# A transformer block scheduled by hand on one core: another order of the loads, another written order and slots, and window copies in two pieces

## The chip, the cores and the metric

One NeuronCore of a Trainium2 chip runs the whole program. The metric is device microseconds of one execution, the median of the runs. Profiles are of one execution each; a profiled execution has a span, from its first to its last instruction, and a time of its own, which is a little longer. PE is the matrix engine, ACT the scalar engine, DVE the vector engine, POOL the general-purpose engine, and SP the engine that here only issues DMA transfers.

## The reference

The block has two gated halves on 2048 tokens of 448 features. A condition vector `c` gives six modulation vectors. The first half is a layer norm, a modulation, and attention with 16 heads of 28 features over a window of 8 tokens at distance 2; the second is a layer norm, a modulation, another layer norm, and an MLP of width 1792.

```python
B, S, D, F, H, Dh, W, dil = 1, 2048, 448, 1792, 16, 28, 8, 2
mod = (silu(c) @ w_mod).reshape(1, 6, 1, -1)
sa, ca, ga, sb, cb, gb = (mod[:, i] for i in range(6))

h = layernorm(x) * (1 + ca) + sa
q, k, v = heads(h @ wqkv)
idx = pos[:, None] - arange(W) * dil            # earlier tokens only
logits = einsum('bhsd,bhswd->bhsw', q, k[idx]) * Dh ** -0.5
o = einsum('bhsw,bhswd->bhsd', softmax(masked(logits)), v[idx])
x = x + ga * (o @ wo)

h = layernorm(x) * (1 + cb) + sb
h = gelu(einsum(layernorm(h), w1) + b1)
x = x + gb * (einsum(h, w2) + b2)
```

## The kernel before

**Tiling.** The 2048 tokens stand as 8 tiles `p` of 128 rows, each row two neighbouring tokens, so that the distance of 2 becomes a distance of 1 within each of two halves `s`. The 448 features are four K tiles: three of 128 rows and a rest of 64, whose matmuls use half of the array's rows. Attention runs in 9 batches of 2·57 queries a half: logits are computed for blocks of 58 queries against 64 keys (`lt`, L733), exponentiated on ACT (L740), masked on DVE (L746), summed (`pd`, L755) and multiplied with v (`po`, L766); the denominators pass twice through ACT (L775, L777) and the scaled result is written by DVE (`qT`, L783) and projected with wo (L798). DVE adds it to x (L805).

**Stages.** Normalised tokens (`zy`, L471) get to feature-major form in two ways: by PE (`ptr`, L528) for the first units, by a DMA transpose otherwise; ACT or DVE then applies the modulation and writes `hT` (L497, L495). Q and K come from `hT`; the first unit's matmuls are at L563 and L541 with the 64-row rest at L547 and go through one PSUM tile `pq` for K and one for Q, each copied to `kT` and `qT` by a cast (L603). Later units produce token-major Q and K, copied to `zy` by ACT or DVE (L622, L623) and transposed by DMA (L625). V of a batch needs the windows of two blocks of 57 tokens, 64 tokens wide each, side by side: the first batch reads `hT` directly (L701), the others read a tile `hw` into which `windows` copies them (L684). Then come x1 = x + attention, two norms, a DMA transpose to `yT` (L829), the first MLP layer (L541 and L547 with `w_s`, `w_r`), gelu on ACT (L859), the second layer (L878), the last add on DVE (L884) and the store (L888). Batches 0–4 are followed by MLP tile 0, 5–6 by tile 1, 7–8 by tiles 2 and 3.

**What sets the order.** `Plan.add` records 703 numbered tasks. `Plan.emit` then issues them in the order of the table `ORDER`; a suffix puts a task on another engine (`:A` ACT, `:D` DVE, `:P` POOL) or takes its variant with the 64-row matmuls first (`:R`), and `k+f@m` issues `f` filler matmuls (`warm_w`, L379) ahead of task `k`. `SLOTS` gives each buffer its slot in its pool, PSUM among them. Each engine, and SP's queue of transfers, works in the order in which its tasks stand in `ORDER`. An argument `after` of `Plan.add` is a constraint on the order that a planner may choose; `emit` makes no instruction from it.

**Loads.** All loads but two tiny ones of `c` are issued by SP. `load` names each load's predecessor:

```python
queue.append(add("SP", 0.5, fn, reads=reads, writes=writes, bufs=bufs, fills=fills, after=queue[-1:], xfer=us,
                 name="load " + writes[0]))
```

The order of definition is x tile 0, `w_mod` for the attention's modulation (`wm_st`, 672 KB, and two rests `wm_r`), three K tiles of the QK weights (`wqk_st`, 225 KB each), x tile 1, two rests of the QK weights (`wqr_st`), x tiles 2–3, V weights, x tiles 4–7, the rest of `w_mod`, wo, and the MLP's. A QK weight is used after a "spread" has copied it into 32-column heads (`Wqk`, L436 on DVE, L438 on ACT, L439 on POOL; `Wqr`, L444 to L447).

Of the kernel before, what the change touches and what calls it, by code (L numbers as in the profile page):

```python
# [15 lines left out]
KT, KS = 4, 64  # L16
# [36 lines left out]
62 61 63+10@63 64 24 25 67 78 79 88:P 26 27 90:A 28 65 86 29 30 91 68+1@68 69 70 80 81 101+8@101 84 82 85:A 83 107  # L53
95+3@95 109 102 93:A 103 96 97 108 110 111 112 94:P 89:P 98 104 105:R 113 114 106 99 100 141 115:D 116 131 129 132 130
133 184 134 31 119:A 120:A 139 140 142 136 143 118:A 117:A 185 179 228:A 180 121 122:R 123 144 135 194 192 137 138 145
146 147 148 149:A 151:A 32 33 34 202 35 36 37 266 195 193 124 125:R 152 276 196 197 150 126 204 203 198 205 206 199
200:D 181 182 156 157 231 232 207 234 186 235 153:R 38 39 165 209 208 166 210 40 201 264 265 277 183 267 158 211 187
229+5@229 154:D 268 167 189 190 236 300 233 237 188 155 239 240 168 301:R 302 274 230:D 275 159 278 160 191 303 306 279
281 269 307 214 304 280 212 282 270 283 41 271 272:A 273 42 171 162:R 163 164 213 215 225 308 305 310 309 238 226 170
169 241 311 312 219:R 313 242 243 244 246 314 315 216 372:A 220 161 284:A 286:A 342 339 287:A 285:A 554:P 217 340 343  # L60
245 247 227 43 44 291:R 292 318 248 288 289 319 316 317 320 341 344 345 347 127 222 223 218 249 250 251 221 373:R 378
321 322 45 348 379 252 375 323 128 324 253 325 328 256 326 376 374 555 556 380 336:P 329 254 257 337:R 338 224 46 47
445:P 48 297 49 50 255 298 258 259 327 330 377 346 381 383 384 261 260 331 262:D 382 332 333 334:D 349 172 385 174 446:R
350 263 447 408 335 351 352 386 354 387 409 413 412 51 424:R 425 52 355 353 176 356 173 414 410 411 426 415 416 53 54
178 357 419:R 359 427 430 431 428 358 175 360 361 364 362 388 389 363 390 391 392 393 177 418 365 481 394 417 395 366
396 397 398 399 440 367 368 400 420 421 293 290 487 448 438 422 423 439 444 488 449 484 451 452 401 402 369 403 370:D
371 485 489 482:R 483 404 441 405 406:D 407 450 453 454 456 486 490 492 294:R 442 295 491 457 455 518:R 458 459 493 494
517 520 521 519 522 495 496 528 532 531 530 460 463 464 461 462 465 497 529 523:R 525 524 527 526 536 537 540 429 539
466 533 498 468 467 469 470 471 473 499 500 501 502 504 534 535 553 590 503 505 432 296 299 506 433 557 560 593 558 559
507 434 435 561 562 509 510 436 594 563 596 595 472 597 474 475 508 511 598 591:R 592 476 547 548 565 566 564 599 512  # L70
477 478 479:D 513 600 514 515 443 437 516 601 549 538 567 602 626 568 550 603 551 604 480 627 628 631 629 605 569 608
609 630 606 632:R 634 633 635 636 543 544 637 641 639 607 640 610 611 638 572 573 642:R 570 571 574 613 612 614 575 577
576 645 615 618 578 579 580 582 581 583 584 616 585 552 541 619 617 620 621 587 643 644 622 623 586 588:D 624 625 542
545 648 656 658 647 659 649 657 660 589 662 663 665 666 680 681 546 646 667:R 664 669 671 668 670 652 650 672 677:R 676
674 673 678 679 675 651 653 691 654 655 685 682 687 688 686 689 690 683 661 699 700 692 693 694 695 684 701 702 696 697
698
# [76 lines left out]
def kernel(  # L153
# [519 lines left out]
    def attention(i, tbl, prev_w1):  # L673
# [5 lines left out]
        if i not in DIRECT:  # L679
            hw = sb("hw", [128, KT, NS, 2, WK], BF16, "hw")  # L680

            def windows(copy):
                h = hT[:, :, kc:kc + WK]
                copy(out=hw.t[:].rearrange("p k s j c -> p (k s) j c"),  # L684
                     in_=bass.AP(h.tensor, h.offset, [h.ap[0], h.ap[1], [WQ, 2], [1, WK]]))
# [271 lines left out]
```

## Time and profile before

| what | value |
|---|---|
| runs | 171.32, 169.91, 171.61 us; median 171.32 |
| profiled execution | 169.7 us, its span 168.0 us |
| busy share of DVE, ACT, POOL | 68%, 63%, 27% |
| DMA | 18.26 MB, 33462 packets, 109 GB/s mean |
| granted TensorE clock, mean | 1.000 |
| gelu, L859, ACT | x56, 33.6 us |
| first MLP layer, L541 with `w_s`, PE | x168, 38.6 us |
| second MLP layer, L878, PE | x238, 44.4 us |
| Q and K, L541 with `wqk_st`, PE | x72, 15.3 us |

In the rows of the profile below, "a<-b" is output and input by the program's names, "128*128" the array's rows and columns in use, "xN" a count. A timeline row gives its start and its duration in us, the engine, the line and the operation; consecutive equal instructions are one row, and the brackets give the engine's idle time before and what ended it. The matmuls' durations overlap those of their neighbours, since they are pipelined, so that the pace of the matrix engine is read from one start to the next. SPq is SP's queue of transfers, where a row is the time of issuing.

### The profile page before, as it was taken

The page shows a single profiled execution, that of the slowest core. Times are in us where ns is not written, and L with a number is a line of the kernel's source. Part 1 is how long each engine was busy: PE and PEld are TensorE (multiplying, and loading weights), DVE is VectorE, ACT ScalarE, POOL GpSimd, SP SyncE. Part 2 cuts the span into 40 slices and gives each one's busy share as a digit, 9 for nine tenths or more (in the row PEclk, how much of TensorE's full clock was granted, in tenths as well). Part 3 has the DMA queues.
Part 4 walks back from the last instruction along what each step waited for, and adds up shares of the span by engine and source line. Part 5 has one row for each costly group of instructions (what it writes and reads, how often), then busy time and mean ns, then how long its engine had stood idle before and what let it go on. Part 6 is the DMA issues. An engine that isn't in the chain of part 4 may idle for free.

```text
span 168.0 us, 4975 instructions
## 1 busy us (share of the span) xinstructions
PE 162.4 (97%) x2116; PEld 84.7 (50%) x2116; DVE 114.4 (68%) x291; ACT 106.5 (63%) x146; POOL 45.7 (27%) x74
## 2 busy tenths in 40 slices
PE   7998999999999999999999999999999999999992
PEld 4785745565444643455544445464343554435571
DVE  7769999878999899997455979855998311002032
ACT  3369998899989835897992896880554404716000
POOL 7143320402616002931008210420123802900000
PEclk9999999999999999999999999999999999999999
DMA  5999949699997997008162000183000610000113
GB/s 159 342 286 385 238 97 155 169 116 149 297 220 181 177 279 124 4 0 96 37 116 68 0 4 4 55 91 92 4 0 0 118 62 0 4 0 0 55 64 102
DMA packets 33462, 18.26 MB, mean 109 GB/s; under 512 B 26395, under 2 KB 32480, under 8 KB 33440
## 3 DMA queue, kind: packets, MB, share of 16 engines
q1 hardware_dynamic: 33436, 17.95, 49.4%
q8 instruction: 16, 0.26, 0.6%
q14 instruction: 6, 0.05, 0.1%
q10 hardware_dynamic: 4, 0.00, 0.0%
HBM read 9.81 MB, written 1.84 MB: 69 GB/s over the span
## 4 chain that ended last, share of the span: by engine, by line
PE 91%; DMA 3%; DVE 2%; ACT 2%; issue 0%; DVEq 0%
PE p L878 26%; PE p L541 22%; PE pq L541 11%; PE pw L798 5%; PE pv L541 5%; PE p L547 4%; PE lt L733 4%; PE po L766 3%; PE pq L547 3%; DMA yT<-zy 3%; PE ps_c L379 2%; PE pd L755 1%; PE pv L547 1%; PE pv L701 1%; PE ptr L528 1%; PE pq L563 1%
## 5 line engine op out<-in xcount | busy, mean ns | idle before, releaser
L859 ACT ACTIVATE hm<-p,b_col 128x512 bf16<-128x512 f32 x56 | 33.6, 696 | 33.0 <-PE p L547 32.4
L878 PE MATMUL p<-w_s,hm 128*128 128x448 bf16 (+1 forms) x238 | 44.4, 342 | 0.0
L541 PE MATMUL p<-yT,w_s 128*128 128x512 bf16 x168 | 38.6, 379 | 0.3 <-DMA yT<-zy 0.3
L878 PEld LDWEIGHTS <-hm 128*128 128x128 bf16 x238 | 22.9, 98 | 19.2 <-issue 0.2
L467 POOL TENSOR_TENSOR rs_all<-tv_all,neg_half 128x2 f32<-128x2 f32 x22 | 17.0, 779 | 53.9 <-DVE tv_all L465 46.8
L884 DVE TENSOR_TENSOR x_all<-p,x1p 128x896 bf16<-128x896 f32 (+2 forms) x10 | 8.9, 901 | 30.6 <-PE p L878 30.6
L541 PEld LDWEIGHTS <-w_s 128*128 128x128 bf16 x168 | 15.7, 98 | 21.5 <-issue 4.1
L451 DVE BATCH_NORM_STATS2 stt<-x_all 128x6 f32<-128x448 bf16 x32 | 19.0, 614 | 0.7 <-DMA x_all<-in_A_x_dram 0.6
L740 ACT ACTIVATE et<-lt 128x928 bf16<-128x928 f32 x18 | 16.2, 947 | 3.1 <-PE lt L733 3.1
L836 POOL TENSOR_TENSOR x1p<-x_all,gbb_bc 128x448 f32<-128x448 bf16 x16 | 16.1, 1038 | 0.0
L541 PE MATMUL pq<-wqk_st,hT 128*128 128x448 bf16 x72 | 15.3, 353 | 0.0
L783 DVE TENSOR_TENSOR qT<-po,den 128x912 bf16<-128x912 f32 x9 | 9.9, 1106 | 6.8 <-ACT den L777 6.1
L798 PE MATMUL pw<-wo_s,qT 128*128 128x448 bf16 x64 | 12.9, 352 | 0.0
L746 DVE TENSOR_TENSOR et<-et,mask 128x928 bf16<-128x928 bf16 x18 | 11.3, 634 | 1.6 <-ACT et L740 1.6
L805 DVE TENSOR_TENSOR x_all<-pw,x_all 128x896 bf16<-128x896 f32 x8 | 8.5, 1084 | 4.2 <-PE pw L798 4.2
L622 ACT CAST zy<-pq 128x896 bf16<-128x896 f32 x11 | 10.0, 908 | 1.6 <-PE pq L547 1.4
L541 PE MATMUL pv<-Wv,hw 128*128 128x448 bf16 x48 | 10.5, 354 | 0.0
L814 DVE TENSOR_TENSOR h<-h,mod_bc 128x896 bf16<-128x896 bf16 x16 | 9.8, 622 | 0.3
L541 PEld LDWEIGHTS <-hT 128*128 128x128 bf16 x72 | 6.5, 98 | 6.4 <-issue 1.0
L777 ACT ACTIVATE den<-den,den_bias 128x928 f32<-128x928 f32 x9 | 9.5, 1068 | 0.2
L451 DVE BATCH_NORM_STATS2 stt<-h 128x6 f32<-128x448 bf16 x16 | 9.5, 618 | 0.2
L798 PEld LDWEIGHTS <-qT 128*128 128x128 bf16 x64 | 6.3, 98 | 5.9 <-DVE qT L783 0.3
(117 smaller groups left out, 190.1 us busy)
## 6 DMA issues: line engine op xcount, KB each, us to landing
w_s<-in_B_w_dram SPq DMA_DIRECT2D x7, 224.0 KB, 3.8
out_dram<-x_all SPq DMA_DIRECT2D x7, 224.0 KB
x_all<-in_A_x_dram SPq DMA_DIRECT2D x3, 448.0 KB, 6.0
wmod<-in_w_mod_dram SPq DMA_DIRECT2D x3, 448.0 KB, 9.7
w_s<-in_B_w_dram SPq DMA_DIRECT2D x3, 448.0 KB, 3.7
wqk_st<-in_A_wqkv_dram SPq DMA_DIRECT2D x3, 225.0 KB
wm_st<-in_w_mod_dram SPq DMA_DIRECT2D x1, 672.0 KB, 4.8
x_all<-in_A_x_dram SPq DMA_DIRECT2D x2, 224.0 KB
```

The source lines that it names most:

```text
L451: add("DVE", 0.53, lambda: nc.vector.bn_stats(out=stt[:, w, b, :], in_=src()), reads=reads, bufs=bufs, after=early if w == b == 0 else (), ...
L467: add("POOL", 0.55 + 0.17 * n, lambda: nc.gpsimd.tensor_tensor(out=r, in0=tv, in1=neg_half[:, 0:n], op=ALU.pow), reads=[f"tv{w}_{b0}", "ne ...
L541: nc.tensor.matmul(out(), lhsT=lhs(kt, slice(0, 128)), rhs=rhs(kt, slice(0, 128)), start=first and kt == 0, stop=not first and kt == KT - 2)
L547: nc.tensor.matmul(out(), lhsT=lhs(KT - 1, rows), rhs=rhs(KT - 1, rows), start=first, stop=not first, tile_position=(rows.start, 0))
L622: add("ACT", 0.80, lambda to=to, src=src: nc.scalar.copy(out=to(), in_=src()), bufs=[pq, st], reads=["zpad"], writes=[(st, 0)], name="evac ...
L740: exps.append(add("ACT", 0.83, lambda half=half, lt=lt: nc.scalar.activation(out=et.t[:, 2 * half:2 * half + 2].rearrange("p r m c -> p r ...
L746: nc.vector.tensor_tensor(out=ev, in0=ev, in1=mask[:], op=ALU.mult)
L783: nc.vector.tensor_tensor(out=qT[:, :, LEAD + q00:LEAD + q00 + 2 * WQ], in0=po.t[:, :, 0:NS * 4 * WQ].rearrange("p j (m c) -> p m j c", c=WQ),
L798: nc.tensor.matmul(pw.t[:, s, 0:D], lhsT=qT[:, KT * s + ft, LEAD + 128 * p:LEAD + 128 * p + 128], rhs=wo_s[:, ft, :], start=(ft == 0), sto ...
L836: add("POOL", 1.0, lambda n=n: nc.gpsimd.tensor_tensor(out=x1p.t[:, n, :], in0=xn(p, n), in1=gbb2_bc[:], op=ALU.add), reads=[f"x{p}", "gbb ...
L859: gelus.append(add("ACT", 0.585, lambda f=f, a=a, p1=p1s[g]: nc.scalar.activation(out=hm.t[:, f].rearrange("p n c -> p (n c)"), in_=p1.t[: ...
L878: nc.tensor.matmul(p2.t[:, n, 0:c1 - c0], lhsT=hm.t[:, f, n, q * 128:(q + 1) * 128], rhs=w2_s[:, f, c0:c1], start=(f == parts[0][0]), stop ...
```

## The change

Three things are changed: `load` lets every load from the fifth on depend only on the fourth; `windows` makes two copies of 128x512 in place of one of 128x1024; and the tables `ORDER` and `SLOTS` are others throughout, with the same 703 tasks.

```diff
     def load(fn, us, writes, bufs=(), reads=(), fills=()):
-        queue.append(add("SP", 0.5, fn, reads=reads, writes=writes, bufs=bufs, fills=fills, after=queue[-1:], xfer=us,
+        queue.append(add("SP", 0.5, fn, reads=reads, writes=writes, bufs=bufs, fills=fills, after=queue[-1:] if len(queue) < 4 else queue[3:4], xfer=us,
                          name="load " + writes[0]))
...
             def windows(copy):
-                h = hT[:, :, kc:kc + WK]
-                copy(out=hw.t[:].rearrange("p k s j c -> p (k s) j c"),
-                     in_=bass.AP(h.tensor, h.offset, [h.ap[0], h.ap[1], [WQ, 2], [1, WK]]))
-
-            add("DVE", 0.37, lambda: windows(nc.vector.tensor_copy), port=True, reads=["pads"] + [f"h{kt}_{p}" for kt in range(KT) for p in ps_],
+                for j in range(2):
+                    copy(out=hw.t[:].rearrange("p k s j c -> p (k s) j c")[:, :, j], in_=hT[:, :, kc + j * WQ:kc + j * WQ + WK])
+
+            add("DVE", 0.46, lambda: windows(nc.vector.tensor_copy), port=True, reads=["pads"] + [f"h{kt}_{p}" for kt in range(KT) for p in ps_],
                 bufs=[hw], fills=[hw], name="windows",
-                alt={"ACT": (0.93, lambda: windows(nc.scalar.copy)), "POOL": (1.1, lambda: windows(nc.gpsimd.tensor_copy))})
+                alt={"ACT": (1.12, lambda: windows(nc.scalar.copy)), "POOL": (1.18, lambda: windows(nc.gpsimd.tensor_copy))})
...
 ORDER = """
-3 0 1 2 11 12 4 9 5 17 14 18 15 55+14@55 19 20 21 10 7 8 13 6 71 22 23 92:P 87:P 73 74 16 56 57 58 72 75 59 60 76 77 66
+15 3 7 0 17 18 19 1 13 5 8 9 20 2 6 10 14 21 73 24 74 11 4 12 71 55+5@55 72 16 56 57 75 76 58 77 59 78 79 61 62 67 60
```

Lines of the changed kernel stand one or two numbers lower (the store is L886, the cast of Q and K L602).

**SP at the start of the program.** Before, the ten loads after x tile 0 follow their definition; `wqk_st` is a K tile of the QK weights, `wqr_st` their rest, `x_all` tokens, `Wv` the V weights:

```order
L336 DMA x_all_68<-in_A_x_dram 128x896
L343 DMA wm_st_135<-in_w_mod_dram 128x3x896
L346 DMA wm_r_157<-in_w_mod_dram 64x448 x2
L322 DMA wqk_st_160<-in_A_wqkv_dram 128x900 x3
L336 DMA x_all_68<-in_A_x_dram 128x896
L326 DMA wqr_st_237<-in_A_wqkv_dram 64x900 x2
L336 DMA x_all_68<-in_A_x_dram 128x2x896
L330 DMA Wv_74<-in_A_wqkv_dram 128x3x448
```

The changed kernel's queue at the same place:

```order
L335 DMA x_all_68<-in_A_x_dram 128x896
L342 DMA wm_st_127<-in_w_mod_dram 128x3x896
L345 DMA wm_r_129<-in_w_mod_dram 64x448 x2
L321 DMA wqk_st_154<-in_A_wqkv_dram 128x900
L335 DMA x_all_68<-in_A_x_dram 128x896
L321 DMA wqk_st_154<-in_A_wqkv_dram 128x900
L325 DMA wqr_st_225<-in_A_wqkv_dram 64x900
L321 DMA wqk_st_154<-in_A_wqkv_dram 128x900
L331 DMA Wv_74<-in_A_wqkv_dram 64x448
L325 DMA wqr_st_225<-in_A_wqkv_dram 64x900
L331 DMA Wv_74<-in_A_wqkv_dram 64x448
L335 DMA x_all_68<-in_A_x_dram 128x2x896
```

Token tile 1 moves ahead of two of the three QK weights, and one rest of these ahead of the last of them; the two small V rests move ahead of token tiles 2–3.

**ACT in the first QK units.** `kT` and `qT` are the casts of K and Q, `hT` the modulated tokens (the first three or four are of token tile 1), `et` the exponentials of batch 0, `vb0` its V. Before:

```order
L460 ACTIVATE tv_all_108<-mvs_107,eps_col_92 128x2
L462 ACTIVATE rs_all_109<-tv_all_108 128x2
L603 CAST kT_71<-pq_274 128x8x128
L603 CAST qT_70<-pq_290 128x8x128
L497 ACTIVATE hT_69<-ptr_338,mod_col_94 128x2x128
L497 ACTIVATE hT_69<-ptr_341,mod_col_94 128x2x128 x2
L497 ACTIVATE hT_69<-ptr_338,mod_col_94 128x2x128
L740 ACTIVATE et_397<-lt_353 128x928
L684 COPY hw_416<-hT_69 128x1024
```

In the changed kernel:

```order
L459 ACTIVATE tv_all_108<-mvs_107,eps_col_92 128x2
L445 COPY Wqr_73<-wqr_st_225 64x256
L461 ACTIVATE rs_all_109<-tv_all_108 128x2
L602 CAST kT_71<-pq_271 128x8x128
L496 ACTIVATE hT_69<-ptr_317,mod_col_94 128x2x128
L496 ACTIVATE hT_69<-ptr_314,mod_col_94 128x2x128
L496 ACTIVATE hT_69<-ptr_317,mod_col_94 128x2x128
L602 CAST qT_70<-pq_291 128x8x128
L714 CAST vb0_112<-pv_362 128x32x28
L738 ACTIVATE et_448<-lt_412 128x928
```

The cast of Q moves behind the modulation of token tile 1, and V's cast ahead of the first exponentials; the window copy leaves ACT at this place. On PE the K half of the first unit's products is now finished whole, then token tile 1 is transposed, then the Q half follows, then the first batch's V, then its logits; before, both halves were finished ahead of these transposes and the first half of the logits stood ahead of V. Fillers are 14, 10, 1, 8, 3 and 5 before and 5, 14, 13 and 5 now.

**SP at the end of the program.** Each row with `out_0_dram` is a store of finished rows; 128x896 is a whole tile of 224 KB, 128x224 a quarter of it. Before:

```order
L888 DMA out_0_dram<-x_all_68 128x896
L829 DMA_TRANSPOSE yT_2746<-zy0_97 128x8x128
L829 DMA_TRANSPOSE yT_2746<-zy4_101 128x8x128
L888 DMA out_0_dram<-x_all_68 128x896 x4
L888 DMA out_0_dram<-x_all_68 128x448
L888 DMA out_0_dram<-x_all_68 128x224 x2
```

In the changed kernel:

```order
L827 DMA_TRANSPOSE yT_2751<-zy3_100 128x8x128
L886 DMA out_0_dram<-x_all_68 128x896 x4
L886 DMA out_0_dram<-x_all_68 128x448
L886 DMA out_0_dram<-x_all_68 128x224
L886 DMA out_0_dram<-x_all_68 128x896
L886 DMA out_0_dram<-x_all_68 128x224
```

A store of a whole tile, that of tile 5 (task 661), now stands between the last two small ones. The window copies are on DVE three times, POOL three times and ACT twice before; now on DVE three times and on POOL five times, each as two instructions. Two more casts of token-major Q and K (L622 in the new numbering, L623 in the old) are on DVE and two fewer on ACT.

More of the change, by code (lines that the diff above doesn't have):

```diff
@@ L56 @@
[L56 to L60, printed above, removed]
@@ new lines @@
+157 154:D 231 232 233 234 235 264 207 165 41 166 236 209 201 187 188 208 210 158 189 190 159:R 160 300:P 237 239
+229+5@229 155 39 266 265 277 274 267 268 275 306 278 191 230 269 279 270 303 167 40 280 304 307 162:R 37 271 336 211 281
+272:D 215 214 127 212 213:A 240 282:D 238 168 38 273 128 308 305 50 283 301 302 216:R 241 309 161 163 311 445 310 170
+169 46 219:R 217:D 242 312 164 313 314 243 246 220 221 337 315 244 247 316 245 342 318 372:P 248 249 339 287:A 286:A
+284:A 285:A 288:R 317 319 320 321 338 291 343 218 45 344 340 289 375 251 250 378 341 323 252 376 379 322 225:R 44 253
@@ new lines @@
+453 406 442 489 454 482:R 486 456 457 590 294 490 483:D 371 492 295:D 407 493 517 491 455 458 518:R 521 522 520 494 495
+496 519 497 459 536 539 528 531 529 498 499 500 501 502 532 460 461 523:R 504 530 527 463 462 464 503 524 525 429 538
+505 506 533 534 465 507 591:R 592 537 508 509 510 466 468 526 511 467 469 540 535 512 428 470 473 471 472 296 514 434
+435 553 299 560 557 561 558 596 597 562 432 433 559 563 593 547 548 598 565 594 436 595 566 599 474 475 513 476 477 478
+515:A 601 564 600 602 626 567 603 549 550 551 604 605 608 609 479 568 606 607 610 569 437 516 480 570 627 629 630 628
@@ L77 @@
+572 632:R 631 633 634 541 542 637 635 636 642:R 543 571 573 574 575 576 577 578 641 639 643 579 582 580 581 638 611 613
+612 614 615 618 583 584 585 616 586 617 587 619 588:D 620 621 623 622 624:A 544 589 645 649 658 648 644 640 659 656 657
+443 660 545 625 662 663 666 667:R 665 664 671 668 669 670 652 653 672 676 674 673 680 677:R 647 678 679 646 684 682 681
+683 650 651 654 691 655 675 687 688 685 552 546 686 689 692 693 699 690 694 700 695 701 702 661 696 697 698
 """
```

28 lines of the change are left out of this document (9 added, 19 removed), and 12 rows, old and new, of the table SLOTS.

## The prediction

> **What bounds the kernel now.** I read the page's busy times and slices first, then every wait of PE that the view of waits lists.
>
> ```profile
> span 168.0 us, 4975 instructions
> PE 162.4 (97%) x2116; PEld 84.7 (50%) x2116; DVE 114.4 (68%) x291; ACT 106.5 (63%) x146; POOL 45.7 (27%) x74
> PE   7998999999999999999999999999999999999992
> ```
>
> ```profile
> PE ps_c L379 <- DVE warm_w L243: 1.3, 1, 1.3
> PE lt L733 <- ACT qT L603: 0.6, 1, 0.6
> PE ps_col L407 <- DVE wm_d L415: 0.3, 1, 0.3
> PE p L541 <- DMA yT<-zy: 0.3, 1, 0.3
> ```
>
> PE is busy 162.4 of 168.0 us. The 5.6 us left are the 1.3 us before its first instruction, three waits of 0.6 + 0.3 + 0.3 = 1.2 us, and about 3.2 us behind its last one. So the matrix engine bounds the kernel nearly throughout, and an order that keeps the same matmuls can win only from these 5.6 us, from fillers and from the cost of changing the shape of the array; it can lose anything. But busy PE time isn't all useful: some of the start is fillers, which PE does because nothing else is ready. The start, from the timeline of PE:
>
> ```profile
> 1.26 3.17 PE L379 MATMUL ps_c<-warm_w 128*128 128x256 bf16 x14 [1.26 <-DVE warm_w L243]
> 4.36 0.60 PE L386 MATMUL ps_c<-one,c_row 1*128 1x128 bf16 x4
> 4.90 1.62 PE L379 MATMUL ps_col<-warm_w 128*128 128x256 bf16 x10
> 7.95 0.61 PE L528 MATMUL ptr<-ident,zy 128*128 128x128 bf16 x8
> 8.40 1.04 PE L379 MATMUL pq<-warm_w 128*128 128x256 bf16 x8
> 9.27 0.38 PE L563 MATMUL pq<-hT,Wqk 128*128 128x256 bf16 x2
> ...
> 9.82 1.25 PE L563 MATMUL pq<-hT,Wqk 128*128 128x256 bf16 x10
> ...
> 13.07 0.62 PE L528 MATMUL ptr<-ident,zy 128*128 128x128 bf16 x8
> 14.28 0.44 PE L733 MATMUL lt<-qT,kT 28*64 28x58 bf16 x32 [0.59 <-ACT qT L603]
> 14.65 1.64 PE L701 MATMUL pv<-Wv,hT 128*64 128x448 bf16 x16
> 16.22 0.83 PE L541 MATMUL pq<-hT,Wqk 128*128 128x256 bf16 x6
> ```
>
> The third place to look at is the stage from 16 to 56 us, where the next engines are also nearly full (a window's row: stretch, its length, busy time of PE, PEld, DVE, ACT and POOL with counts, clock, DMA share, GB/s):
>
> ```profile
> 16.20:30.00 13.80, 13.80 (x280) 8.05 (x277) 13.64 (x38) 13.06 (x16) 3.42 (x7) 1.00 0.91 176
> 30.00:45.00 15.00, 15.00 (x332) 8.17 (x331) 12.55 (x26) 14.41 (x19) 4.13 (x6) 1.00 0.96 168
> 45.00:56.50 11.50, 11.50 (x260) 5.67 (x258) 11.29 (x32) 10.59 (x13) 4.56 (x5) 1.00 0.96 224
> ```
>
> There DVE is busy 13.64 + 12.55 + 11.29 = 37.5 of 40.3 us, 2.8 us short of full, and PE doesn't wait once.
>
> **The start.** Work to be done by the end of the first unit: the first half of QK unit 0, token tile 1's transposes, the second half, V, the logits. Before, the next QK unit begins at 16.22, with 0.44 us of batch 0's logits still to come behind it; after, these come ahead of it, so 16.66 is the comparable time. A walk through the new order, step by step: the modulation's matmuls wait for `silu_bc` and end about where they did, so the first transposes start at 8.05 (an estimate; 7.95 before) and take 0.45 (8.40 − 7.95). Then come 13 fillers at the pace of the row at 8.40, (9.27 − 8.40) / 8 = 0.109 us, to 9.9; before, two QK matmuls and all fillers are done at 9.82.
>
> ```profile
> 8.16 1.16 POOL L439 COPY Wqk<-wqk_st 128x512 bf16<-128x512 bf16 x2 [3.76 <-DMA wqk_st<-in_A_wqkv_dram]
> 12.30 1.01 ACT L603 CAST kT<-pq 128x1024 bf16<-128x1024 f32 x1 [1.13 <-PE pq L541]
> 13.21 1.02 ACT L603 CAST qT<-pq 128x1024 bf16<-128x1024 f32 x1
> 14.12 1.95 ACT L497 ACTIVATE hT<-ptr,mod_col 128x256 bf16<-128x256 bf16 x4
> ```
>
> POOL now makes three of these spreads instead of two, at 0.58 each, so the third ends near 8.16 + 3 × 0.58 = 9.9, in time for the second K tile. The stretch with the K half is 18 of the unit's 32 matmuls, 0.11 us each, and ends near 11.9. Tile 1's transposes (0.45) and the 14 others (1.5), with 0.2 for changes of shape, take PE to about 14.1, V (1.6 by its row) to 15.7. Meanwhile ACT casts K (1.0), modulates three quarters of tile 1 (0.49 each) and casts Q (1.0): 11.9 + 1.0 + 1.5 + 1.0 = 15.4, before V is done. The logits, 2 × 0.4 us, end at 16.5, and 16.66 is to be compared with it. The wait of 0.59 for the cast of Q goes, since V now covers it; what is late next are the fillers, which stand in the order whether or not data come sooner. Token tile 1 lands earlier, but DVE has it only behind the modulation columns and the casts behind PE's K half. I take 0. From the walk's roughest step, whether the third spread is in time, the bounds are ±0.6, the size of the wait that goes.
>
> **Shapes.** PE loses 0.10 us where a group ends with other rows in use: in the chain, six matmuls of the same size take 1.24 us ahead of a change and 1.14 without.
>
> ```profile
> 52.30 1.24 PE pv L541 x6
> 53.55 1.14 PE pq L541 x6
> ```
>
> Along the new order there are 88 such changes, before 90: −0.2.
>
> **The full stage.** DVE loses one cast of V (1.09) and two tail copies there later, and gets one more cast of token-major K (1.06), one more window copy, and a weight spread. Its own rows for the windows:
>
> ```profile
> L684 DVE COPY hw<-hT x3: 396/424/426, 26.6 to 100.0; 128x1024 bf16<-128x1024 bf16 x3
> L684 POOL COPY hw<-hT x3: 1037/1038/1042, 43.1 to 52.3; 128x1024 bf16<-128x1024 bf16 x3
> L684 ACT COPY hw<-hT x2: 1028/1055/1082, 16.8 to 38.4; 128x1024 bf16<-128x1024 bf16 x2
> L436 DVE COPY Wqk<-wqk_st 128x512 bf16<-128x512 bf16 x2 | 0.5, 286 | 0.0
> L719 DVE CAST vb<-pv 128x896 bf16<-128x896 f32 x1 | 1.1, 1092 | 0.0
> L623 DVE CAST zy<-pq 128x896 bf16<-128x896 f32 x1 | 1.1, 1059 | 0.0
> ```
>
> Two halves cost at least the 0.42 of the whole copy, and at most, by the row of another copy of 128x512, 2 × 0.286 = 0.57; I take 0.07 more than the whole, for halves that follow each other without a gap. The sum of DVE's tasks up to the last one that feeds the first MLP tile comes to +0.6 us, up to the batch's last scaling to +0.8. It fits into the 2.8 us that are idle, but the wait of 0.3 for `yT` shows that the chain of norms has no margin at its end. Nearest rows: −0.3 (that wait gone) to about +1.8 (below). I take 0, because in both orders the output projections of two tiles still stand on PE between the last scaling and the first MLP product. The first copies on POOL take 1.04 us each; PE needs them at V, more than a batch after, so they hide; without that cover each would cost up to its 1.04. On ACT two window copies (2.1 us) and two casts go: ACT isn't waited for in this stage, so no gain.
>
> **The end.**
>
> ```profile
> 163.00:165.00 2.00, 1.84 (x17) 1.40 (x15) 1.05 (x3) 0.00 (x0) 0.00 (x0) 1.00 0.62 229
> L888 SPq DMA_DIRECT2D out_dram<-x_all x10: 332/332/517, 87.6 to 165.3; - x10
> DMA to landing us min/median/max: 1.6/1.6/1.6
> 164.87 0.39 DVE L884 TENSOR_TENSOR x_all<-p,x1p 128x224 bf16<-128x224 f32 x1 [0.35 <-PE p L878]
> ```
>
> The last add ends at 165.26, and its store is issued at once, takes 0.33 to issue and lands 1.6 later. Now the 224 KB store of tile 5, issued before, stands between the last two small ones. Its rows have been ready for long, so it waits for the small store ahead of it, which comes from an add of 0.39 us that ends near 164.7; it then takes its 0.33 of SP's time until about 165.4, and the last store can only be issued from there: +0.1 to +0.33. If its bytes also go first through the 16 DMA engines, that is more: the DMA share of 0.62 in 2 us is 1.24 us for two whole tiles before, 0.62 each. So the ends are +0.25 (issue alone, with the queue's small steps) and +0.65; I take +0.45, halfway, since issue and bytes partly overlap. The Trainium skill's "DMA: Bandwidth & Descriptors", "Queues, rings and completion order", says that on each DMA engine the descriptors of one queue are taken in ring order; by it the sum would carry the upper end, 0.65. The profile has no case of a large store just ahead of the last one, so it can't say.
>
> **Sum**: 0 − 0.2 + 0 + 0.45 = +0.25 on the profiled execution's 169.7 us, so 169.95. The median of the runs, 171.32, is 1.6 above that execution, and I put the difference on the median: 171.57, rounded to 171.5.
>
> **Rivals.** A difference within 1%, 1.7 us, is about what a measurement of this kernel can't tell from no change.
>
> *Everything that waits goes (faster).* The waits of 0.6 + 0.3 + 0.3 go, four fillers fewer (41 to 37) are 0.44 at 0.109, the shapes 0.2, and the large store fits between two issues: −1.85, 169.5. For it: the wait list holds these waits and each has a changed step ahead of it. Against: fillers are cheap only if data are early, and each wait of the start ended at a step that has its own chain. 0.14.
>
> *Half pace at the start (slower).* PE's first 14 fillers took (4.36 − 1.26) / 14 = 0.221 us each, those at 8.40 0.109: the pace doubled in the second group, about 4.2 us after the first matmul. Only 5 fillers now stand ahead of `c`; they end at about 2.4, and PE is idle until `c` has landed. If the fast pace needs an unbroken run and counts again from a gap, the last gap being ahead of the transposes near 8.0, then it comes at 8.0 + 4.2 = 12.2: the 13 fillers cost 13 × 0.11 = 1.4 more, the K half 0.6 to 1.2 more, of which 0.5 lies in fillers that waited anyway: +1.8 net of the shapes, and +0.45 at the end, so 173.5. It decides if the half pace reaches past 9.5. Against it: the fillers of the row at 4.90 pass through a gap-free stretch, and 14 of the new ones fill the same. 0.13. The Trainium skill's "TensorE: Matmul & The Clock Gate", "Part 1: The HAM clock gate", has the clock go up after a busy window of about 3.4 us that runs freely; the rows' 4.2 us agree with it roughly, though the profile's mean granted clock is 1.000 with them in it. By it the 14 fillers would open the clock before 8.0, and this rival would not come about.
>
> *DVE's stage is late (slower).* The +0.8 on DVE lands in full on the wait for `yT`, and the two more window copies of POOL hold up short DVE rows:
>
> ```profile
> 43.14 1.04 POOL L684 COPY hw<-hT 128x1024 bf16<-128x1024 bf16 x1 [1.76 <-ACT hT L497]
> 43.88 0.32 DVE L465 TENSOR_SCALAR tv_all<-mvs 128x2 f32<-128x2 f32 x1
> L465 DVE TENSOR_SCALAR tv_all<-mvs x22: 158/169/714, 14.6 to 128.4; 128x2 f32<-128x2 f32 x22
> ```
>
> While POOL copied, that row took 0.32, not its usual 0.17, and the worst 0.71. Two copies at up to 0.54, less the part in DVE's idle time, are 0.5; the chain of scaling and `wo` meets the delay once more at batch 2, 0.5. Sum 0.8 + 0.5 + 0.5 − 0.2 + 0.45 = +2.0: 173.3. It decides when DVE's task sum grows by more than the idle time ahead of each consumer; speaking for it, DVE is at 13.64 of 13.80 in the first stretch, and against it, at 12.55 of 15.00 in the second. 0.22.
>
> *The loads come no earlier.* Tile 1's bytes share the DMA engines with the weights ahead of them, and if it lands no sooner the start is as before. That gives 0 there too, and it lies in the forecast.
>
> **The numbers.** Forecast, within 1%: 0.51, its own range 169.8 to 172.6 (start ±0.6, DVE −0.3 to the edge of 1%, end 0.25 to 0.65). Faster 0.14; slower 0.13 + 0.22 = 0.35. The range reaches down to the faster rival's 169.5 in part, 169.6, and up past both slower ones' 173.5 by a little, 173.8; what is left out is half of the faster case and the slower cases beyond their price.
>
> **What would show it.** Start: the second QK unit's first matmul at 16.66 ± 0.6, no wait for the cast of Q; half pace would show as fillers 0.22 apart behind 8.0. The full stage: the waits of PE keep at most 0.3 for `yT`; the third rival would show there as waits for `yT` or for scaled tokens of over 0.5. The end: from the last add's end to the end of the span, 168.0 − 165.26 = 2.7 before, 3.2 after. I am wrong if PE's busy time itself changes by more than 1 us, since the same matmuls at the same pace are assumed; or if a wait shows up in the MLP phases, where the order is also new and I have counted nothing.

## The result and the profile after

| | median, us | runs | lowest to highest |
|---|---|---|---|
| before | 170.82 | 20 | 169.76 to 173.82 |
| changed | 171.85 | 20 | 170.68 to 175.12 |

The ratio is 1.0061, 95% interval 1.0037 to 1.0085: 1.0 us slower (0.6 to 1.5), inside 1%. The highest times are those of a few slower executions, which the ratio leaves out. The profiled execution of the changed kernel took 171.82 us, its span 170.1. That of before, at 169.7, is faster than every one of its 20 other runs, while the changed kernel's is close to its median, so the spans (168.0 and 170.1) show about twice the difference of the medians. A second profile of the order before, in the experiment with split copies, has a span of 168.8.

The page of the changed kernel and all waits that the view of PE's waits lists:

```profile
span 170.1 us, 4976 instructions
PE 162.8 (96%) x2112; PEld 84.2 (50%) x2112; DVE 120.5 (71%) x295; ACT 103.9 (61%) x144; POOL 47.2 (28%) x80
PE 83%; DMA 6%; DVE 4%; SPq 2%; issue 1%; ACT 1%; POOL 1%; DVEq 0%
```

```profile
PE ps_c L378 <- DVE warm_w L242: 1.3, 1, 1.3
PE pq L546 <- DVE b_col L664: 1.1, 1, 1.1
PE pq L562 <- ACT hT L496: 0.8, 1, 0.8
PE ps_c L385 <- DMA c_row<-in_c_dram: 0.6, 1, 0.6
PE po L764 <- DVE qT L781: 0.2, 1, 0.2
```

PE is nearly as busy as before (162.8 against 162.4 us): the time went into waits, and of the chain (the third row of the page) 6% now runs through DMA and 2% through SP's queue, before 3% and none. The three old waits (the cast of Q, the modulation's weights, `yT`) are gone. New are a wait of 1.1 us in the full stage and one of 0.2 at `po` behind it, and at the start one of 0.8 and one of 0.6, in which PE waits for `c` behind the five fillers. The start, from PE's timeline:

```profile
1.26 1.25 PE L378 MATMUL ps_c<-warm_w 128*128 128x256 bf16 x5 [1.26 <-DVE warm_w L242]
3.09 0.60 PE L385 MATMUL ps_c<-one,c_row 1*128 1x128 bf16 x4 [0.58 <-DMA c_row<-in_c_dram]
3.62 3.17 PE L378 MATMUL ps_col<-warm_w 128*128 128x256 bf16 x14
7.77 0.61 PE L527 MATMUL ptr<-ident,zy 128*128 128x128 bf16 x8
8.21 1.58 PE L378 MATMUL pq<-warm_w 128*128 128x256 bf16 x13
10.55 1.32 PE L562 MATMUL pq<-hT,Wqk 128*128 128x256 bf16 x8 [0.75 <-ACT hT L496]
17.17 0.83 PE L540 MATMUL pq<-hT,Wqk 128*128 128x256 bf16 x6
```

The second QK unit begins at 17.17, 0.51 behind 16.66. The first MLP product begins at 63.24, before at 61.17, so that the stage between loses another 1.56; what follows it loses 0.03. The full stage, in the windows of before (the first one from its own second QK unit on):

```profile
17.17:30.00 12.83, 12.83 (x249) 7.76 (x242) 11.82 (x34) 11.21 (x15) 5.33 (x12) 1.00 0.70 142
30.00:45.00 15.00, 13.68 (x263) 6.82 (x261) 12.33 (x26) 12.51 (x16) 1.30 (x2) 1.00 1.02 190
45.00:56.50 11.50, 11.40 (x319) 5.90 (x319) 11.37 (x34) 10.43 (x13) 5.05 (x8) 1.00 1.11 261
```

PE loses 1.32 us between 30 and 45. DVE isn't fuller than before there (12.33 against 12.55), but the column of DMA is (it sums packet times that overlap, so that it can pass 1): 1.02 and 1.11, before 0.96 and 0.96, while the first stretch is emptier, 0.70 against 0.91. So transfers moved later. Which ones, SP's queue shows, with POOL's tail copy that completes token tile 5, and DVE's next work on it:

```profile
28.46 0.29 POOL L482 COPY zy<-zy 128x128 bf16<-128x128 bf16 x1 [4.37 <-DVE zy L470]
```

```profile
25.84 1.32 SPq L624 DMA_TRANSPOSE kT<-zy  x1
27.21 1.36 SPq L362 DMA_DIRECT2D wo_s<-in_A_wo_dram  x1
28.67 0.57 SPq L641 DMA_DIRECT2D mod_hbm<-mod_rows  x1
29.29 0.88 SPq L362 DMA_DIRECT2D wo_s<-in_A_wo_dram  x2
30.28 1.25 SPq L519 DMA_TRANSPOSE zT<-zy  x1
```

```profile
35.24 1.06 DVE L494 TENSOR_SCALAR hT<-zT,mod_col 128x512 bf16<-128x512 bf16 x3 [2.32 <-DMA zT<-zy]
36.31 0.17 DVE L664 CAST b_col<-pb 128x14 f32<-128x14 bf16 x1
```

Tile 5's tokens are ready at 28.75, and its transpose (`zT`, L519) is issued at 30.28: behind the store of the modulation rows and two loads of wo, a third of which SP had issued just ahead. DVE stands idle for 2.32 us until the transpose has landed, and PE's 1.1 us, put down to `b_col`, the last of the instructions that DVE does then, is the end of that. Before, the four loads of wo were issued together at a time when no transpose was due:

```profile
13.99 3.22 SPq L363 DMA_DIRECT2D wo_s<-in_A_wo_dram  x4
22.57 1.33 SPq L520 DMA_TRANSPOSE zT<-zy  x1
24.00 1.27 SPq L625 DMA_TRANSPOSE qT<-zy  x1
25.36 1.39 SPq L520 DMA_TRANSPOSE zT<-zy  x1
```

### The profile page after: what moved, and what is told of

Read it like the earlier page. It is cut to its first block, busy times and chain, and to the rows that moved or that the text cites. A ratio compares the mean times of both kernels' runs of the same rounds, so it can differ in the third digit from the quotient of the medians.

```text
span 170.1 us, 4976 instructions
## 1 busy us (share of the span) xinstructions
PE 162.8 (96%) x2112; PEld 84.2 (50%) x2112; DVE 120.5 (71%) x295; ACT 103.9 (61%) x144; POOL 47.2 (28%) x80
## 4 chain that ended last, share of the span: by engine, by line
PE 83%; DMA 6%; DVE 4%; SPq 2%; issue 1%; ACT 1%; POOL 1%; DVEq 0%
PE p L876 25%; PE p L540 22%; PE pq L540 9%; PE pw L796 7%; PE pv L540 4%; PE p L546 4%; DMA wqk_st<-in_A_wqkv_dram 3%; DMA zT<-zy 3%; PE lt L731 3%; PE po L764 2%; PE pq L546 2%; PE pd L753 1%; DVE et L744 1%; PE pv L546 1%; DVE stt L450 1%; PE pv L699 1%
## 5 line engine op out<-in xcount | busy, mean ns | idle before, releaser
L466 POOL TENSOR_TENSOR rs_all<-tv_all,neg_half 128x2 f32<-128x2 f32 x22 | 16.5, 757 | 45.7 <-DVE tv_all L464 36.8
L812 DVE TENSOR_TENSOR h<-h,mod_bc 128x896 bf16<-128x896 bf16 x16 | 11.3, 714 | 0.4
L683 POOL COPY hw<-hT 128x512 bf16<-128x512 bf16 x10 | 5.8, 613 | 18.9 <-PE pv L546 18.9
L773 ACT ACTIVATE den<-pd 128x928 f32<-128x928 f32 x9 | 8.5, 950 | 1.5 <-PE pd L753 1.4
```

Of the source, the lines that this page charges most:

```text
L466: add("POOL", 0.55 + 0.17 * n, lambda: nc.gpsimd.tensor_tensor(out=r, in0=tv, in1=neg_half[:, 0:n], op=ALU.pow), reads=[f"tv{w}_{b0}", "ne ...
L812: add("DVE", 0.55, lambda vec=vec, op=op: nc.vector.tensor_tensor(out=h2.t[:], in0=h2.t[:], in1=vec.unsqueeze(1).to_broadcast([128, NS, D] ...
```

## The experiments

Ratios are to the kernel before, timed on the same chip. "QK" is the start of the second QK unit, "MLP" that of the first MLP product, both from the profile of the run; orders that have half of the first batch's logits behind QK are to be read 0.44 later in the column QK (marked *).

| run | ratio, 95% interval | span, us | QK | MLP |
|---|---|---|---|---|
| before | | 168.0 | 16.22* | 61.17 |
| changed | 1.0061 (1.0037 to 1.0085) | 170.1 | 17.17 | 63.24 |
| a1_loads | 1.0108 (1.0070 to 1.0147) | 171.4 | 17.40 | 64.52 |
| a2_store | 1.0071 (1.0037 to 1.0105) | 170.1 | 16.40 | 63.24 |
| a3_zt5 | 1.0070 (1.0028 to 1.0112) | 169.9 | 16.36 | 63.02 |
| b1_split | 0.9976 (0.9956 to 0.9995) | 168.8 | 16.60* | 62.02 |
| c2_po3 | 1.0085 (1.0059 to 1.0111) | 170.0 | 16.79 | 63.14 |
| c3_both | 1.0054 (1.0024 to 1.0083) | 169.1 | 16.71 | 62.19 |
| g_122 | 1.0221 (1.0194 to 1.0249) | 172.7 | 17.89 | 65.89 |
| d1_fill | 1.0118 (1.0086 to 1.0151) | 170.2 | 17.65 | 63.36 |
| f1_wo | 0.9992 (0.9974 to 1.0010) | 168.4 | 17.08 | 61.53 |
| f2_all | 1.0010 (0.9990 to 1.0031) | 168.9 | 17.08 | 62.00 |
| f4_lt | 1.0008 (0.9989 to 1.0027) | 168.5 | 16.31* | 61.71 |
| m1_wo | 1.0127 (1.0103 to 1.0151) | 170.4 | 16.24* | 62.73 |

In these kernels a line of the code can stand one or two numbers off those above.

**a1_loads**: the first loads of the changed kernel in the order of before. Its tasks on SP, with tile 1's statistics and ACT's copy moved so that they don't block:

```diff
-wqk0, x1, wqk2, wr0, wqk1, wvr1, wr1, wvr0, x2
+wqk0, wqk1, wqk2, x1, wr0, wvr1, wr1, wvr0, x2
```

> The changed kernel with the first loads in the order of before (three QK weights, then token tile 1, then the QK rests), tile 1's statistics on DVE behind tile 0's modulation, and ACT's copy of the QK rest behind it too. Theory: tile 1's tokens and a QK rest ahead of the last QK weight are what delays the first QK products (0.75 us wait at 9.80, 0.11 at 11.15); the second QK unit then begins at 16.5 to 16.7 instead of 17.17 and the time falls by about 0.5 us, ratio to before near 1.003. Rival: tile 1's tokens come 1.5 us later and its transposes become what is waited for; the second unit stays at 17.2 or later, ratio 1.006 or more.

QK at 17.40, ratio 1.0108: no gain, so the theory fell. The rival's numbers came, but not its mechanism: PE didn't wait for tile 1, but 0.30 us for ACT's copy of the QK rest. Eight profiles share the changed kernel's order up to there (a2, a3, c2, c3, g, f1, f2 and its own); they have QK at 16.36 to 17.89, on average 16.94. Before, b1 and m1 share the other one, at 16.66 to 17.04 with the 0.44, on average 16.79. What the eight differ in is when the weights land: POOL began the first of its spreads at 10.21 in g, which has the latest QK, at 9.18 in the changed kernel's own profile, and at 8.46 to 8.77 in the four with the earliest (a2, a3, c2, c3).

**a2_store**: the end of the written order with the large store back in its place.

```diff
-693 699 690 694 700 695 701 702 661 696 697 698
+693 699 690 661 694 700 695 701 702 696 697 698
```

> The changed kernel with the large store of tile 5 moved back ahead of the last three small ones. Prediction's term: 0.45 us faster (0.25 to 0.65), and the span ends about 2.3 us behind the last add instead of 2.73. Rival, from the profile of the changed kernel, where the end behind the last add is as long as before: the large store is issued and gone before the last add ends, so nothing changes, 0 within 0.1 us in the profile.

The span is 170.1 again, and in the changed kernel the end behind the last add is what it was before:

```profile
166.99 0.39 DVE L882 TENSOR_TENSOR x_all<-p,x1p 128x224 bf16<-128x224 f32 x1 [0.95 <-PE p L876]
```

167.38 to 170.1 is 2.7, and 165.26 to 168.0 was 2.7. DVE now waits 0.95 between the last two adds, 0.35 before, and in that gap, at 166.45 to 166.87, the large store is issued. The rival held: 0.

The same profile shows something else. The first wait in the full stage is there (1.0 us), and a second, at `po`, put down to "issue", a name for waiting on nothing that the profile shows:

```profile
PE po L765 <- issue: 1.0, 1, 1.0
PE pq L547 <- DVE b_col L665: 1.0, 1, 1.0
```

```profile
53.36 0.39 PE L754 MATMUL pd<-et,ones_k 64*32 64x464 bf16 x8
53.57 1.09 PE L765 MATMUL po<-et,vb 64*32 64x57 bf16 x107
55.70 0.27 PE L765 MATMUL po<-et,vb 64*32 64x57 bf16 x21 [1.04 <-issue]
```

QK was 0.77 us earlier than in the changed kernel's own profile, and yet the first MLP product starts at 63.24 in both: the gain was swallowed at 55.70, where PE goes on in both.

**a3_zt5**: the transpose of tile 5 (task 211) ahead of wo's loads.

```diff
-229+5@229 155 39 266 265
+229+5@229 155 211 39 266 265
...
-167 40 280 304 307 162:R 37 271 336 211 281
+167 40 280 304 307 162:R 37 271 336 281
```

> The changed kernel with the DMA transpose of token tile 5 issued ahead of four other transfers of SP (two pieces of wo and the store of the modulation rows among them). Theory: it was queued behind them, issued 1.5 us after its tokens were ready; it is now issued near 28.8 instead of 30.28, lands by 33.7, and PE's wait of 1.13 us at 35.4 falls to 0.3 or less; about 1 us faster, ratio to before near 1.000. Rival: one DMA engine that is busy with a 16 KB instruction packet, or the full DMA engines, set the landing; the wait stays at 0.8 or more, or comes back within the next batch, and the time falls by 0.3 us at most.

The wait of 1.1 went, and the first output projection began at 38.26 instead of 39.75 in a2 at the same QK. The time didn't fall: transposes of Q and K of the next batches, which also stand behind these loads on SP, were late instead, and the stop at `po` was there.

```profile
PE po L765 <- issue: 0.9, 1, 0.9
PE ps_c L386 <- DMA c_row<-in_c_dram: 0.8, 1, 0.8
PE lt L732 <- DMA qT<-zy: 0.7, 1, 0.7
PE lt L732 <- DMA kT<-zy: 0.6, 1, 0.6
```

So the place of one transpose isn't the cause; the rival was right that the wait comes back.

**b1_split**: before, with the two copies of the changed `windows`, and nothing else.

> The kernel before with the window copies split in two and nothing else. Forecast: hidden, within 0.2 us of before; a pair on DVE takes 0.49, on POOL about 1.1 to 1.2, on ACT 1.2 to 1.3 us. Rival: the longer holds on DVE and POOL delay the chain of norms in the full stage, 0.3 to 0.8 us slower, seen as a longer wait for yT.

0.9976, no slower. The rows of the copies are 0.286 us each on DVE, 0.616 on POOL and 0.634 on ACT; the two of a pair overlap by up to 0.15, so that from the start of the first to the end of the second a pair takes 0.46 to 0.49, 1.17, and 1.12 to 1.17:

```profile
L684 DVE COPY hw<-hT x6: 261/286/293, 26.9 to 101.1; 128x512 bf16<-128x512 bf16 x6
L684 POOL COPY hw<-hT x6: 612/616/618, 43.9 to 53.9; 128x512 bf16<-128x512 bf16 x6
L684 ACT COPY hw<-hT x4: 602/634/663, 17.1 to 39.5; 128x512 bf16<-128x512 bf16 x4
```

A pair is a little longer than the one copy, by 0.07 us on DVE, 0.13 on POOL and 0.09 on ACT on average, and hidden. That it is a gain I don't claim: the interval ends just below 1, the span isn't shorter, and f4_lt, which has the split too, is at 1.0008.

**c2_po3**: in the changed order, `po` of batch 3 (task 346) behind one group of V matmuls; **c3_both**: that, tile 5's transpose as in a3_zt5, and one MLP load (46) behind the transposes of Q and K of batches 3 and 4.

```diff
-381 382 256 53 328 326 329 327 330 292 223 554:P 290 346 555:R 254 383
+381 382 256 53 328 326 329 327 330 292 223 554:P 290 555:R 346 254 383
```

> The changed kernel with the second of two batches' `po` products in a row moved behind one group of V matmuls. Theory: PE runs out of instructions there. In three of four profiles of this order it stops at the same instruction (the 108th of 128 `po` matmuls), 1.2 to 1.5 us after a 16 KB instruction packet has ended, whatever came before; the packet is fetched 256 PE instructions ahead, and pd, po, po are 272 short ones in a row. With 16 slow matmuls between, the stop of about 1.0 us goes and the time falls by 0.5 to 1.0 us, ratio to before 1.001 to 1.004. Rival: what the profile calls issue is a wait for data that comes when it comes; the stop only moves to V or to the output projection, ratio 1.006 to 1.007 as before.

> The changed kernel with token tile 5's transpose issued early, one MLP weight load moved behind the transposes of Q and K of batches 3 and 4, and the second `po` moved as in the kernel of this name. Theory that the two causes (SP's order ahead of the transposes, and the fetch) are separate and together make up the loss: both waits of about 1 us go, the waits for Q and K of 0.70 and 0.57 fall below 0.4 each; ratio to before 0.995 to 1.000. Rival: the stage is bound by the DMA transposes themselves, so PE waits for the next of them; ratio 1.002 to 1.006.

In c2 the stop is gone, as in every profile with that edit (c3, f2), and PE waits 0.3 us at V instead; two more changes of shape would cost 0.2 at the 0.10 of the prediction (an estimate). From QK to the first MLP product it takes 46.35, against 46.84 in a2: half a microsecond, of which the runs show nothing, since the ratio of 1.0085 isn't below the changed kernel's. The gain that was expected of it didn't come, though the stop went. c3 brings this to 45.48 and the span to 169.1, with waits of 0.08, 0.32 and 0.31 left. So the waits fell as its theory had it, but the ratio, 1.0054, is in the rival's range and isn't told apart from the changed kernel's.

**g_122**: the start of the changed order and its slots, up to the second QK unit, followed by the order of before, with split copies.

> The kernel before with the start of the changed one (its order up to the first half of the second QK unit, its first loads among it) and split window copies. Theory: the start is worth 0.3 to 0.6 us (second QK unit at 16.4 in two profiles of the changed order, against 16.66 to 17.04 for the same work before) and the loss comes later, from the order behind it; ratio to before 0.995 to 0.998, with the split copies' 0.998 in it. Rival: the gain at the start is lost to DVE and the transposes in the full stage, ratio 1.000 or more.

It fell, far: QK at 17.89, behind a wait of 1.4 us for the spread weights, 0.5 + 0.2 at the next transposes, 0.5 at a `po` (at 32.4) and 1.1 for `yT`. About 1 us of the loss is the late start, which the order itself doesn't explain, since seven others with it are earlier; the rest comes behind it, in the order of before. Why it waits there wasn't tried further; the start is at any rate not a part that brings a gain ahead of any order.

**d1_fill**: 14 and 10 fillers in place of 5 and 14.

```diff
-55+5@55 ... 63+14@63
+55+14@55 ... 63+10@63
```

> The changed kernel with 14 fillers ahead of the condition's matmuls and 10 ahead of the modulation's, as before, in place of 5 and 14. If the gap of 0.6 to 0.9 us behind 5 fillers delays the full pace (0.215 us from filler to filler until 6.4 us or later in the changed kernel, until about 5.5 before), the full pace comes by 5.7 again; the modulation's matmuls then start at 6.4 instead of 6.7 to 6.9, and the second QK unit 0 to 0.3 us earlier. Rival: the pace doesn't decide there, since the matmuls wait for the condition and for the spread weights; second QK unit at 16.4 or later, time unchanged within 0.2 us.

The pace does depend on them:

```profile
1.26 3.17 PE L379 MATMUL ps_c<-warm_w 128*128 128x256 bf16 x14 [1.26 <-DVE warm_w L243]
4.36 0.54 PE L386 MATMUL ps_c<-one,c_row 1*128 1x128 bf16 x4
4.83 1.26 PE L379 MATMUL ps_col<-warm_w 128*128 128x256 bf16 x10
7.28 0.61 PE L407 MATMUL ps_col<-silu_bc,wm_st 128*128 128x32 bf16 x18 [1.19 <-DMA wm_st<-in_w_mod_dram]
```

The second group runs at 1.26 / 10 = 0.13 us or less from its first filler on, where in the changed kernel all 14 fillers at 3.62 are (6.65 − 3.62) / 14 = 0.22 apart. But the modulation's matmuls waited 1.19 us for their weights here, the first QK products 0.8 for the spread weights, and QK came at 17.65, as the rival had it. The time wasn't lower (1.0118), so the pace doesn't decide; why this one is slower than the changed kernel the runs don't settle.

**f1_wo**: the changed kernel with only the four loads of wo back behind the modulation weights and the load of b1. SP's queue:

```diff
 load wmod2 (four pieces), load b1
+load wo 0, 1, 2, 3
 transposes zT4, tq2, tk2
-load wo 2
 store of the modulation rows
-load wo 3, load wo 0
 transpose zT5, broadcast of the modulation rows
-load wo 1
 transpose zT6
```

> The changed kernel with the four loads of wo issued behind the modulation weights, near 14 us, as before, in place of 27 to 32 us between the DMA transposes. Theory: these loads are what token tile 5's transpose queues behind on SP; its issue falls from 30.28 to near 29, the wait of 0.95 to 1.13 us at 35 us falls to 0.3 or less, the first output projection starts at 38.3 to 39 instead of 39.75 to 40.7; the stop in the `po` products stays (about 1 us, or more, since PE comes there earlier), so the time gains 0 to 0.4 us. Rival: the transposes set their own time on the DMA engines; the wait stays at 0.8 or more.

0.9992: the whole loss is gone, where 0 to 0.4 us of it had been expected. SP's queue, DVE's work on tile 5 and the complete list of PE's waits:

```profile
13.26 4.97 SPq L363 DMA_DIRECT2D wo_s<-in_A_wo_dram  x4
...
27.25 0.56 SPq L642 DMA_DIRECT2D mod_hbm<-mod_rows  x1
28.68 1.24 SPq L520 DMA_TRANSPOSE zT<-zy  x1
```

```profile
32.75 1.05 DVE L495 TENSOR_SCALAR hT<-zT,mod_col 128x512 bf16<-128x512 bf16 x3
```

```profile
PE ps_c L379 <- DVE warm_w L243: 1.3, 1, 1.3
PE ps_c L386 <- DMA c_row<-in_c_dram: 0.9, 1, 0.9
PE pq L563 <- POOL Wqk L439: 0.3, 1, 0.3
```

Behind the start no wait is listed at all. The transpose is issued 1.6 us earlier, and DVE has tile 5 2.5 us earlier and without an idle moment ahead of it; the 0.9 beyond the issue mean that it also landed sooner behind it. From QK to the MLP it takes 44.45, before 44.51. Matmul by matmul against the changed kernel's own profile, 1.3 us are won at the wait put down to `b_col` and 0.3 at the `po` behind it, and from there on the two keep their distance. The stop at the later `po` is 0.11 us here and 0.10 in that profile, so it has no part in this gain.

**f2_all**: f1_wo, with the edits of c3_both that concern `po` and the MLP load.

> The kernel with wo's loads early, and besides the second `po` behind a group of V matmuls and one MLP weight load behind the transposes of Q and K of batches 3 and 4. Theory of two causes: PE's waits between the second QK unit and the first MLP product sum to 0.7 us or less (2.2 in the changed order, 0.3 before), the profile's span is 168.5 to 169.0, ratio to before 0.997 to 1.002. Rival: a further transpose or DVE becomes what is late, span 169.5 or more, ratio 1.004 or more.

1.0010, span 168.9: as the theory had it, but not better than f1_wo, since moving `po` leaves the 0.3 us wait at V and wo's place alone had already done the rest.

**m1_wo**: the mirror of f1_wo, the kernel before with wo's loads late.

```diff
 load wmod2 (four pieces)
-load wo 0, 1, 2, 3
 transposes zT4, tq2
+load wo 2, 3, 0
 transpose zT5, store of the modulation rows, transpose tk2, broadcast
+load wo 1
 transpose zT7
```

> The kernel before, with the loads of wo moved to where the changed kernel has them: three of them ahead of token tile 5's transpose, one behind the modulation's broadcast. If that place alone makes the transposes late, a wait of 0.3 to 1.2 us appears between 28 and 40 us, or that for yT grows, and the time rises by 0.3 to 1.0 us, ratio 1.002 to 1.006. If it needs the rest of the new order (the transpose later needed, or DVE fuller), nothing changes, ratio 0.998 to 1.001.

1.0127, 2.2 us slower and more than the expected 0.6%: this edit alone costs more in the old order than the whole change does. The two largest that are new in its list of waits:

```profile
PE lt L733 <- DMA kT<-zy: 0.7, 1, 0.7
PE po L766 <- issue: 0.6, 1, 0.6
```

The transpose of K behind the moved loads is late, which costs 0.8 us at 32.7. Another 0.8 comes from a stop at a `po` at 37.8, of which neither b1_split nor the kernel before has one listed; it is in an earlier batch than the stop at 55.7 in a2. The last 0.5 or so appears only at 82 us, where PE waits for a mask of DVE; by what way the loads reach that far isn't shown.

**f4_lt**: the kernel before with split copies and V of batch 0 (task 179) ahead of its logits (184).

> The kernel before with split window copies and V of the first batch ahead of its first logits, as the changed kernel has it. Theory: the wait of 0.59 us for the cast of Q is covered by V's 1.6 us and goes; ratio 0.994 to 0.996. Rival: DVE and ACT behind it get the logits 1.2 us later, and the exponentials and masks push the gain back into a wait before the first MLP product; ratio 0.998 or more.

The rival's ratio came: 1.0008. The wait of 0.6 us only changed its name: V waits for the cast of Q as the logits did, since its PSUM slot is the one that the cast empties. In the changed order V's slot is the one that the cast of K empties, and that has ended at about 14.0 when V starts at 14.96; there the wait is gone.

## Why the prediction came out as it did

The forecast was 171.5 us, 0.25 us slower than before, within 1%; measured are 1.0 us slower, within 1%, and inside the range. The bound was read rightly (PE's work is the same, only waits could change), but two terms of the sum were off, in opposite directions. That the direction is right is luck: it rested on the end's +0.45 alone, which came out as 0, and without it the sum said −0.2; the loss came from a term that was set to 0. That 171.5 lies so near the 171.85 is luck in part, too: the forecast was put on a median of three runs, 171.32, which lies half a microsecond above that of 20.

- **Start, 0 ± 0.6.** Right: 16.94 against 16.79 on average, well inside the scatter (a single profile of each, 17.17 against 16.66, would have said 0.5). The steps were partly others. The Q cast's wait went as said. But the walk had POOL's three spreads end one behind the other at 9.9; in the changed kernel's profile the third ends at 11.2, and ACT's copy of the QK rest waits 1.7 us for its load with the modulation of tile 0 queued behind it, a queue that I didn't walk. The move of the tokens ahead of two QK weights, the change's headline, is worth nothing that these runs can show.
- **Shapes, −0.2.** Misread, though small. The 90 and 88 count every change of rows or columns between neighbouring matmuls; of rows alone, at which the 0.10 was read, the two profiles have 80 before and 82 after, so the term should have been +0.2. Neither is shown by itself.
- **Split copies, about 0.07 a pair on DVE, hidden.** Right: 0.48 to 0.50 for a pair on DVE in the changed kernel, 1.17 on POOL, and no loss in b1_split.
- **Full stage, 0, with 1.8 as the other end.** This is the step that failed. The size of the loss, 1.56 in the two profiles, lies in those bounds, but the term was argued from DVE's sum of tasks and the rival from DVE's delay. DVE wasn't it: its busy time between 30 and 45 us fell. I had priced the loads only at the start, where the diff names them, and not the ones of wo, which the free order let slip from 14 us to 27 to 32 us, onto SP's queue and the DMA engines among the transposes. From QK to the first MLP product the changed order took 46.07 and 46.84, the order before 44.51 and 44.98; f1_wo gives it all back with this one edit (44.45), and m1_wo makes it in the old order (46.05). That the place of these loads is the cause is shown from both sides. What isn't separated is how much of it is SP's time for issuing them and how much the bytes among those of the transposes: of the 2.5 us by which DVE has tile 5 sooner in f1_wo, 1.6 are the earlier issue.
- **End, +0.45.** Wrong, 0: the working took the time between the last two adds from before, and the last groups of matmuls stand in another order now, with 0.95 us of DVE's idle time between the adds in place of 0.35. The page of the Trainium skill on DMA ("DMA: Bandwidth & Descriptors", "Queues, rings and completion order"), by which the sum would have carried the upper end of 0.65, isn't contradicted: the large store is issued at 166.45, before the last add begins at 166.99, and no run here shows the case it speaks of.
- **Rival of the half pace.** It didn't come about: in the changed kernel's own profile the transposes at 7.77 are (8.21 − 7.77) / 8 = 0.055 us apart, as before at 7.95 with (8.40 − 7.95) / 8 = 0.056, and no fillers 0.22 apart stand behind 8.0. Part of its mechanism is there. With 14 fillers ahead of `c` (before, b1, d1, f4, m1) PE reaches the full pace between 4.2 and 5.7 us. With 5, three of nine profiles (the changed kernel's own, c2, g) have it at their first transposes, at 7.8 to 8.0, and six reach it only at 8.3 to 9.3, but none near the rival's 12.2, so the count doesn't begin again at the last gap. It costs little since the matmuls there wait for data anyway: in a2_store QK came at 16.40 with the full pace from 8.4. The Trainium skill's "TensorE: Matmul & The Clock Gate", "Part 1: The HAM clock gate", has a busy window of about 3.4 us that runs freely; by it the prediction had the 14 fillers open the clock before 8.0, and the traces agree with that in three of the nine profiles and not in the other six.
- **Rival of DVE's stage.** The right place, at twice the measured size (+2.0 against 1.0 of the medians), by another cause. Its sign, waits over 0.5 us in the full stage, appeared, and would have been read as that rival's; only moving wo's loads tells the two apart.

What stays open is the stop at `po`. It falls on the same matmul, the 108th of 128, with 1.29 (a1), 1.04 (a2) and 0.88 us (a3), but with 0.10 in the changed kernel's own profile and 0.11 in f1_wo. In d1_fill, with wo's loads late as in these and five more fillers ahead, it isn't there, nor with slow matmuls put among the short ones (c2, c3, f2). So that it comes with wo's loads isn't shown. The page counts 16 packets of "instruction", 0.26 MB, for the 2112 matmuls and 2112 weight loads of PE's program, so about one packet per 264 of them:

```profile
q8 instruction: 16, 0.26, 0.6%
```

In the five profiles that stop at the 108th matmul, PE goes on 1.25 to 1.5 us behind the end of such a packet; in d1_fill the packet had ended about 2 us before these products began. This fits a PE that has run out of fetched instructions; no view shows the wait itself, so it is argued and not shown.

## What to carry to other kernels

When an order of transfers is set free, list every transfer that changed its place against its neighbours on the issuing queue, and not only those that the change is about: the four that cost the time were nowhere near the ones that it was made for. A load with slack belongs where the queue and the DMA engines have slack, even if it is needed much later; put among transfers that others wait for, it can delay all behind it, as both f1_wo and m1_wo show. And where removing a wait doesn't move the time, as with one transpose here, the wait may be a sign of a queue that is late as a whole.

## What was not expected of the hardware

- A load of 98 KB took SP 0.3 to 0.6 us to issue as a rule, but single ones 1.3 to 1.5: one at 27.2 us of the changed kernel, among transposes, and one at 14.7 us of the kernel before, ahead of every transpose. So it isn't the transposes alone that hold them up. A transpose took SP 1.2 to 1.4 us as a rule, and up to 2.2 in these two profiles.
- The same first 16 us, with PE's instructions in the same order, ended between 16.36 and 17.89 us in eight profiles, largely by when the first weights landed. A difference of half a microsecond between two single profiles of a start says nothing.
- Five matmuls and then a gap of 0.6 to 1.0 us, in place of 14 matmuls without one, put off PE's full pace by 2 to 5 us: it is reached at 7.8 to 9.3, against 4.2 to 5.7.
